# Sliding-window attention and token MLP: softmax terms of two row groups interleaved in memory, masks moved to GpSimd as 4-byte products, normalise allowed on GpSimd

## The chip, the cores and the metric

One core of one Trainium2 chip. The metric is device time in microseconds (us) of one execution. A kernel is timed in rounds beside the kernel before on the same chip, and every ratio below is the mean time of one kernel's fast runs over that of the other's fast runs of the same rounds, with its 95% interval, so it is not quite the ratio of the medians that are quoted. A kernel counts as faster or slower if that interval lies wholly beyond 2%, as the same if wholly within, and as unclear otherwise. One profiled execution of each kernel gives its trace. A run of this program on one core can also come out slow at a lower granted TensorE clock (`dense_wrong`: 521.8 us at a clock of 0.944, its three other runs 512.56 to 516.25 us at 0.954 to 0.963); only fast runs are compared, and it is said where a profile fell into the slow state.

## The reference, cut to what matters

```python
def _A_ref(x, wqkv, wo):                       # attention, 32 heads of 16, window 256
    B, S, D = x.shape                          # 1, 2048, 512
    H = 32; Dh = D // H; W = 256
    ...
    scores = jnp.einsum("bhqd,bhkd->bhqk", q, k) * (Dh ** -0.5)
    idx = jnp.arange(S)
    mask = (idx[:, None] - idx[None, :] >= 0) & (idx[:, None] - idx[None, :] < W)
    scores = jnp.where(mask[None, None], scores, -1e9)
    p = _softmax(scores, axis=-1)
    o = jnp.einsum("bhqk,bhkd->bhqd", p, v)
    ...
def _B_ref(x, w1, b1, w2, b2):                 # MLP over the tokens, 2048 -> 1792 -> 2048
    ...
def reference(A_x, A_wqkv, A_wo, B_x, B_w1, B_b1, B_w2, B_b2):
    x = A_x
    x = x + _A_ref(_layernorm(x, axis=-1), A_wqkv, A_wo)
    x = x + _B_ref(_layernorm(x, axis=-1), B_w1, B_b1, B_w2, B_b2)
    # ... and both once more with the same weights
```

## The kernel before: the parts that matter

The kernel is a list of 2,531 operations on five engines. The order in which they are issued, and the engine for those that may run on several, is a packed table made offline (`ORDER`); each operation carries an estimated `cost` that the offline search used and the chip never sees. `op("vector:mask", ..., alts=[("gpsimd", ...)])` means VectorE or, if the table says so, GpSimd.

Scores of eight heads (four row groups, `r` = 0 to 3, of two heads each) are made by four matmuls for each block of 64 keys, into four PSUM banks; most tiles hold two or three blocks. Two exponentials on ScalarE, each over a pair of banks (`i` = 0, 1; up to 512 columns each), write bf16 into a tile `pt` in SBUF, one row group after the other. Masks set the terms outside the window to zero by a product with 0/1, in place. Then eight small matmuls for each block take `pt` as the moving operand ("probability matmuls" below).

```python
pt = sb("pt", [P, NPT, 4, 512])                # bf16: tile, row group, column
...
op("scalar:exp", lambda e, ...: e.activation(
    pt[:, tp.slot, 2 * i:2 * i + 2, 0:cols], pair(ts)[:, :, 0:cols],
    ACTF.Exp, scale=SMSCALE), reads=[ts, "acttab"], writes=[(tp, i)], cost=act_cost(2 * cols))
...
def f_mask(e, ...):
    v = pt[:, tp.slot, :, c0 * 64:c0 * 64 + w]
    msk = ldm[:].rearrange("p a b -> p (a b)")[:, w0 * 64:w0 * 64 + w]
    if n == 1:
        return e.tensor_tensor(v, v, msk.unsqueeze(1).to_broadcast([P, 4, w]), op=ALU.mult)
    ...
nm = 4 * n * nc_ * 64
op("vector:mask", f_mask, reads=keys + LD, writes=keys, cost=dve_cost(nm, 0.5), lock=True,
   alts=[("gpsimd", f_mask, 100 + 2.03 * nm)])
...
last = e.matmul(..., lhsT=vb[...], rhs=pt[64 * h:64 * h + 64, tp.slot, r, base + c0 * 64:base + (c0 + n) * 64], ...)
...
def normalise(t):                              # (x - mean) * root, 512 columns, bf16
    op("vector:xh", lambda e: e.tensor_scalar(xh_sb[:, t, :], x_sb[:, t, :], agg[:, t, 0:1], rstd[:, t, :],
                                           op0=ALU.subtract, op1=ALU.mult), ..., lock=True)
```

The softmax here doesn't subtract the row's maximum and nothing guards it: scores larger than these inputs give would overflow.

## Time and profile before

| | kernel before |
|---|---|
| median of the first 3 runs | 479.63 us (478.91 to 480.4) |
| span of the profiled run, granted clock | 476.5 us, 0.988 |
| exponentials back to back, start to start | 0.904 us for 1,024 elements a partition |
| GpSimd mask back to back, 512 / 256 elements | 1.13 / 0.63 us |
| VectorE mask back to back, 512 elements | 0.34 us (mean duration 0.60) |

"Start to start" is the median spacing from an instruction to the next one on the same engine, taken where the engine was idle for under 30 ns between them; it is what an instruction costs its queue. A recorded duration is longer than that (here by some 25 to 140 ns): the records of neighbours overlap, as with the full-size exponentials of before, recorded at a mean of 1,054 ns and 904 ns start to start.

One line of the page of the kernel before gives the busy time of each engine in us, its share of the span and its instructions (PEld is TensorE's weight load, DVE VectorE, ACT ScalarE, POOL GpSimd):

```profile
PE 421.0 (88%) x6355; PEld 199.2 (42%) x6416; DVE 368.0 (77%) x702; ACT 331.4 (70%) x388; POOL 227.6 (48%) x252
```

By groups of instructions the page gives: line, engine, operation, output and inputs, shapes, count; then busy us and mean ns of one; then the idle time of that engine just before them and what ended most of it:

```profile
L685 ACT ACTIVATE pt<-PS 128x1024 bf16<-128x1024 f32 (+1 forms) x304 | 283.3, 1043 | 27.1 <-PE PS L670 26.4
L695 POOL TENSOR_TENSOR pt<-pt,ldm 128x256 bf16<-128x256 bf16 (+1 forms) x148 | 147.4, 1006 | 74.3 <-ACT pt L685 62.3
L695 DVE TENSOR_TENSOR pt<-pt,ldm 128x512 bf16<-128x512 bf16 (+1 forms) x124 | 69.7, 569 | 9.1 <-ACT pt L685 7.4
...
L493 DVE TENSOR_SCALAR xh_sb<-x_sb,agg,rstd 128x512 bf16<-128x512 bf16 x64 | 34.9, 561 | 2.2 <-POOL rstd L486 2.0
```

L685 is the exponential, L695 the mask, L493 the normalise. Two ways of masking share the work, 148 on GpSimd and 124 on VectorE (four more, for the tail, are on another line).

The chain of work that ended last, as shares of the span by engine:

```profile
PE 50%; DVE 30%; ACT 15%; POOL 2%; issue 2%; DMA 0%
```

Busy times of each engine in four stretches (columns: TensorE matmul, TensorE weight load, VectorE, ScalarE, GpSimd, then granted clock, DMA share and rate). The first and third are attention, the second and fourth MLP:

```profile
22.00:185.00 163.00, 134.66 (x2752) 61.52 (x2752) 149.21 (x266) 138.69 (x157) 105.91 (x110) 0.98 0.25 59
185.00:245.00 60.00, 58.29 (x404) 29.14 (x409) 39.82 (x86) 22.14 (x32) 7.33 (x9) 1.00 0.40 112
245.00:400.00 155.00, 138.05 (x2613) 61.62 (x2637) 133.53 (x248) 141.50 (x158) 101.19 (x108) 0.99 0.21 53
400.00:477.00 77.00, 72.50 (x331) 32.69 (x336) 27.78 (x48) 9.31 (x14) 1.47 (x2) 0.99 0.50 145
```

In the first attention stretch VectorE is nearly full (149 of 163 us); in the second ScalarE is fullest. The MLP stretches belong to TensorE (busy for 58.3 of 60 and 72.5 of 77 us). Of the table of waits (who waited for whom: us in total, times, longest), two lines of the kernel before:

```profile
POOL pt L695 <- ACT pt L685: 62.3, 39, 5.0
...
ACT pt L685 <- PE PS L670: 26.4, 40, 1.8
```

ScalarE waits 26.4 us for scores in all; that is how much faster exponentials could be fed at most.

### The profile page before, as it was taken

Reading aid. Unit: us, or ns where it says so; the run is one execution under the profiler, and the core shown is the slowest. Engines: PE = TensorE matmul, PEld = TensorE weight load, DVE = VectorE, ACT = ScalarE, POOL = GpSimd, SP = SyncE. Lnnn points to the kernel's source line nnn. Section 1 sums busy time; section 2 is a strip of 40 time slices with the busy share of each in tenths; the row PEclk is TensorE's granted clock in tenths of the full one; section 3 lists DMA queues with packets and bytes.
Section 4 is the critical chain, followed back from the end, with each engine's and each line's share of the span. In section 5 each row is a group of like instructions: output and inputs, shape, how many; then the busy total and the mean of one; then the engine's idle time right before and its main releaser. Section 6 shows DMA issues by size and latency. Waiting matters only on the chain.

```text
span 476.5 us, 14658 instructions
## 1 busy us (share of the span) xinstructions
PE 421.0 (88%) x6355; PEld 199.2 (42%) x6416; DVE 368.0 (77%) x702; ACT 331.4 (70%) x388; POOL 227.6 (48%) x252
## 2 busy tenths in 40 slices
...
GB/s 220 136 46 62 144 1 36 126 44 3 3 45 34 92 46 227 165 96 11 89 89 14 91 35 3 3 135 46 3 36 89 47 105 183 132 192 142 100 194 71
DMA packets 79392, 39.77 MB, mean 83 GB/s; under 512 B 20960, under 2 KB 79328, under 8 KB 79328
## 3 DMA queue, kind: packets, MB, share of 16 engines
...
## 4 chain that ended last, share of the span: by engine, by line
PE 50%; DVE 30%; ACT 15%; POOL 2%; issue 2%; DMA 0%
PE PS L512 30%; ACT pt L685 14%; DVE pt L695 8%; PE PS L837 7%; PE PS L670 4%; PE PS L607 4%; PE PS L716 4%; DVE rl L736 3%; DVE xh_sb L493 3%; DVE stats L470 2%; DVE x_sb L758 2%; DVE oT L747 1%; DVE vb L618 1%; POOL pt L695 1%; PE PS L514 1%
## 5 line engine op out<-in xcount | busy, mean ns | idle before, releaser
L685 ACT ACTIVATE pt<-PS 128x1024 bf16<-128x1024 f32 (+1 forms) x304 | 283.3, 1043 | 27.1 <-PE PS L670 26.4
L695 POOL TENSOR_TENSOR pt<-pt,ldm 128x256 bf16<-128x256 bf16 (+1 forms) x148 | 147.4, 1006 | 74.3 <-ACT pt L685 62.3
L695 DVE TENSOR_TENSOR pt<-pt,ldm 128x512 bf16<-128x512 bf16 (+1 forms) x124 | 69.7, 569 | 9.1 <-ACT pt L685 7.4
L512 PE MATMUL PS<-xh_sb,w1b 128*128 128x512 bf16 x262 | 69.2, 389 | 7.4 <-issue 2.4
L670 PE MATMUL PS<-qT,kbd 32*128 32x256 bf16 (+4 forms) x1488 | 61.4, 255 | 12.1 <-DVE rl L736 3.6
L512 PE MATMUL PS<-uT,w2b 128*128 128x512 bf16 x268 | 68.4, 379 | 0.9 <-issue 0.6
L486 POOL TENSOR_TENSOR rstd<-rstd,mhalf 128x2 f32<-128x2 f32 (+1 forms) x33 | 23.3, 712 | 78.5 <-DVE rstd L484 77.0
L864 DVE SCALAR_TENSOR_TENSOR x_sb<-PS,b2col,x_sb 128x512 bf16<-128x512 f32 x32 | 23.3, 747 | 47.8 <-PE PS L512 47.7
L716 PE MATMUL PS<-pt,vb 64*32 64x320 bf16 (+4 forms) x2976 | 44.9, 251 | 16.5 <-DVE pt L695 9.0
L512 PE MATMUL PS<-xhT,wqkv 128*128 128x512 bf16 (+1 forms) x218 | 51.6, 364 | 5.3 <-issue 2.2
L670 PEld LDWEIGHTS PS<-qT,kbd 32*128 32x128 bf16 x1488 | 22.1, 93 | 66.9 <-ACT pt L685 40.7
L852 ACT ACTIVATE uT<-rl,b1col 128x512 bf16<-128x512 f32 x28 | 18.3, 712 | 42.5 <-DVE rl L848 42.5
L736 DVE STREAM_TRANSPOSE rl<-PS 128x1024 f32<-128x1024 f32 x32 | 39.7, 1242 | 8.1 <-PE PS L716 7.8
L470 DVE BATCH_NORM_STATS2 stats<-x_sb 128x6 f32<-128x512 bf16 x64 | 42.9, 681 | 3.3 <-DMA x_sb<-in_A_x_dram 2.8
L716 PEld LDWEIGHTS PS<-pt,vb 64*32 64x32 bf16 x2976 | 28.5, 90 | 35.9 <-issue 11.2
L512 PE MATMUL PS<-uT,pt 128*128 128x512 bf16 x165 | 42.2, 379 | 0.2
L512 PEld LDWEIGHTS PS<-xh_sb,w1b 128*128 128x128 bf16 x280 | 23.0, 99 | 39.1 <-issue 11.1
L512 PEld LDWEIGHTS PS<-uT,w2b 128*128 128x128 bf16 x278 | 25.9, 98 | 31.6 <-issue 2.5
L837 PE MATMUL PS<-xh_sb,w1b 128*128 128x512 bf16 x165 | 37.1, 379 | 1.4 <-DVE xh_sb L493 1.2
L493 DVE TENSOR_SCALAR xh_sb<-x_sb,agg,rstd 128x512 bf16<-128x512 bf16 x64 | 34.9, 561 | 2.2 <-POOL rstd L486 2.0
L742 POOL TENSOR_TENSOR ul<-rl,rc 128x512 bf16<-128x512 f32 x23 | 25.8, 1123 | 22.3 <-DVE rc L740 20.5
L607 PE MATMUL PS<-wqkv,xhT 128*64 128x256 bf16 x512 | 34.0, 275 | 1.3 <-DVE rstd L484 1.3
...
## 6 DMA issues: line engine op xcount, KB each, us to landing
w1b<-in_B_w_dram SPq DMA_DIRECT2D x112, 128.0 KB, 2.7
...
```

Source lines behind the costliest of these rows:

```text
L470: op("vector:stat", lambda e: e.bn_stats(stats[:, t, :], x_sb[:, t, :]), reads=[f"x{t}"], writes=[f"st{t}"], cost=dve_cost(512), after=lat ...
L486: op("gpsimd:rstd", lambda e: e.tensor_tensor(rstd[:, t0:t1, 0], rstd[:, t0:t1, 0], mhalf[:, 0:1].to_broadcast([P, t1 - t0]), op=ALU.pow), ...
L493: op("vector:xh", lambda e: e.tensor_scalar(xh_sb[:, t, :], x_sb[:, t, :], agg[:, t, 0:1], rstd[:, t, :], op0=ALU.subtract, op1=ALU.mult), ...
L512: return e.matmul(o, lhsT=w, rhs=x, start=start, stop=stop, skip_group_check=True)
L607: last = e.matmul(bank(ft)[64 * j:64 * j + 64, sc * 256:(sc + 1) * 256], lhsT=xhT[:, tx.slot, c, tok:tok + 64], rhs=wqkv[:, c, 1024:1536]. ...
L670: last = e.matmul(bank(tt[r // 2], r % 2)[:, base + c0 * 64:base + (c0 + n) * 64], lhsT=kbd[32 * r:32 * r + 32, tk.slot, o, jj].rearrange( ...
L685: op("scalar:exp", lambda e, ts=ts, tp=tp, i=i, cols=cols: e.activation(pt[:, tp.slot, 2 * i:2 * i + 2, 0:cols], pair(ts)[:, :, 0:cols], A ...
L695: return e.tensor_tensor(v, v, msk.unsqueeze(1).to_broadcast([P, 4, w]), op=ALU.mult)
L716: last = e.matmul(bank(t, h)[32 * r:32 * r + 32, i + q0 * 64:i + (q0 + n) * 64], lhsT=vb[64 * h:64 * h + 64, tk.slot, jj, 4 * o + r, :], r ...
L736: op("vector:od", lambda e, t=tod, tr=tr: e.transpose(rl[:, tr.slot:tr.slot + 2].rearrange("p a b -> p (a b)"), pair(t)), reads=[(tod, i) ...
L742: f_n = lambda e, tr=tr, tl=tl: e.tensor_tensor(ul[:, tl.slot].rearrange("p (q x d) -> p x q d", x=2, d=16), T(tr)[:, :, :, 0:16], R(tl).u ...
L837: last = e.matmul(bank(tu, tt), lhsT=v()[:, sc - b0, k0 + tt * P:k0 + (tt + 1) * P], rhs=xh_sb[:, sc, :], start=(sc == b0), stop=(sc == NT ...
```

## The change

Its intent: put two row groups beside each other in memory, so that the bf16 terms of two heads at one column form one 4-byte word with one mask value, and mask both by one int32 product with 0 or 1. Then a mask costs GpSimd half as many elements, all 276 masks go there and VectorE gets rid of them. Normalise may now run on GpSimd, and the table was searched anew offline.

```diff
-    '...'        # ORDER, the packed table: replaced whole (35 lines, cut)
+    '...'
-        ldm = sb("ldm", [P, 4, 64])
+        ldm = sb("ldm", [P, 4, 64], dt.int32)
...              # the memset of the value tile's ones is written as 4-byte words; runs three times, at the start
         def normalise(t):
-            op("vector:xh", lambda e: e.tensor_scalar(xh_sb[:, t, :], x_sb[:, t, :], agg[:, t, 0:1], rstd[:, t, :],
-                                                   op0=ALU.subtract, op1=ALU.mult),
-               reads=[f"x{t}", f"ag{t}", f"rs{t}"], writes=[f"xh{t}"], cost=dve_cost(512, 0.25, ptrs=2), lock=True)
+            f_xh = lambda e: e.tensor_scalar(xh_sb[:, t, :], x_sb[:, t, :], agg[:, t, 0:1], rstd[:, t, :],
+                                             op0=ALU.subtract, op1=ALU.mult)
+            op("vector:xh", f_xh, reads=[f"x{t}", f"ag{t}", f"rs{t}"], writes=[f"xh{t}"], cost=dve_cost(512, 0.25, ptrs=2),
+               lock=True, alts=[("gpsimd", f_xh, pool_cost(512, 2))])
...
+        def probs(t):
+            return pt[:, t.slot].rearrange("p a b -> p (a b)").rearrange("p (i c r) -> p i c r", i=2, r=2)
...
-                            pt[:, tp.slot, 2 * i:2 * i + 2, 0:cols], pair(ts)[:, :, 0:cols],
+                            probs(tp)[:, i, 0:cols, :].rearrange("p c r -> p r c"), pair(ts)[:, :, 0:cols],
...
-                            v = pt[:, tp.slot, :, c0 * 64:c0 * 64 + w]
-                            msk = ldm[:].rearrange("p a b -> p (a b)")[:, w0 * 64:w0 * 64 + w]
+                            v = probs(tp).bitcast(dt.int32)[:, :, c0 * 64:c0 * 64 + w, 0]
+                            msk = ldm[:].rearrange("p a b -> p (a b)")[:, w0 * 64:w0 * 64 + w].unsqueeze(1)
                             if n == 1:
-                                return e.tensor_tensor(v, v, msk.unsqueeze(1).to_broadcast([P, 4, w]), op=ALU.mult)
+                                return e.tensor_tensor(v, v, msk.to_broadcast([P, 2, w]), op=ALU.mult)
...
-                        op("vector:mask", f_mask, reads=keys + LD, writes=keys, cost=dve_cost(nm, 0.5), lock=True,
-                           alts=[("gpsimd", f_mask, 100 + 2.03 * nm)])
+                        op("gpsimd:mask", f_mask, reads=keys + LD, writes=keys, cost=100 + 2.03 * 2 * n * nc_ * 64)
...
-                                            rhs=pt[64 * h:64 * h + 64, tp.slot, r, base + c0 * 64:base + (c0 + n) * 64],
+                                            rhs=probs(tp)[64 * h:64 * h + 64, r // 2, base + c0 * 64:base + (c0 + n) * 64, r % 2],
```

The exponential walks its output row group by row group (`p r c`), so it writes 512 bf16 elements at a step of 4 bytes, and then the 512 between them. The probability matmuls read at the same step.

More of the change, by code (lines that the diff above doesn't have):

```diff
@@ L15 @@
 ORDER = (
-    'c-qZXO=#mt7B1P9v>GZ<feI*44H{5`1{6?(2GpPhHK;)i8t{M`)Sv-1n8gF`#SLn3gBHA?0S&0Z4Ic0z3tsR-',
-    '7P63o7QB#y4?bid10Kl12M^@n1s`(AA%`5iu;t%4{WH^ZSax3=>D7;_>V5BfUkR;*!~noQ08sqB83aPn&|KiUnp6170YHM2iDEu7OJ&n4KKA?O',
-    '=_%!<sMe9H)vELa!u@h(Jh?7RMuAnnaD3Zx3$EpyfYDf%sogX*O%OzayOhAXpj<1$ktiM>3}1-',
-    'CxG%O&vKP<4`R2KJ@2Su}Oly%rjjApP!ZY}+EX#`Qrm1WsiJ2HC3H%2SY_+0EB0m9u?pT(Oh~H@N{P(BCymIONOcVuj&=!u)Yr~<U43v5p3O&O',
-    'x!eW;BLBHQGwx24*v)?otZ%$9sAKL9U#u(IUD0w{=@#y=?zmGF~^p@Z-h7g8E6vatw3<hz0=u>LcUXI5-Tat=p>8G-',
@@ L21 @@
-    'k1sObapLx5k`=Zm_m*ssqZ8Xvp?VFbMt%-',
-    '=P6VnXnb5!~2dAU?k6zS>L+gMiJ!eG#oudpbJzGxVDZ!~&fS&H(LX&U=mO`$F!9IHx<R8^gXQG`N_$|@@Qfuc~V={tn*J48G<*xkL>uJ*|VAq*',
-    '^{$ZDFBQ&p+yx~?ce&>8q!n$`e~v~};^ZX=2!N0KDnxOZ?*Py|U<cp{3FiZUh&&x>LxN#pTYy}TUpiXy80vt5P`Pdf;J4iMVDAhh?Hp{*^1&;g',
-    '3$*!QccSGUqq7&eRTcC+;DpOBn3d2#Yuj_WD)aNLfa0U<A60&@N8RfWd2QjO>NF!cR!Jg$bSB!%*L{EWB7NaQ8geN=hmW}Zu_@0a{iP?o<gInK',
-    'j}I{Q(cC$etqI?rQFc>(bgG~s1Qz1$ULIZ0Byb4sdGSSU!+KTV$)qPV-OD0eab3{yk}!LnEf(yp$kJQ2n$VgSana?W2|T;Ksdr<5{pXNOmRM(7',
@@ L26 @@
-    'No9sZ=pR_%7XDbL5pe>=AAs_nY1@87mstuieg(eG+Sx*s*A@Ku<mX&8o4tn0NJPBg4ir5Z*i<|R}vshT(#rjHP^PK~lGN!H%p-',
-    'UDHXkSt=X_Ita>s-',
-    'm(=K}3`d1+mzJ?Yk}}l4uc=Y*Vw+ZaXaPMAdd;72Ares0x}IPXQ3AyuH0m>G{RQiPS6bosKNsMJI?S1U5!@@4~4mQ5MG+ldCMLw)t-',
-    'LsL_WQv+f|^vEnMQ;E4!Q2z82~&O@jcTvPW{ElE^`hn@fn0>O<23?Yz;AW&^jEtx?<bqcZw1QAlP(*ej31fnS>p`I&gQq9psLWw5&Y@hx8=;#R',
-    'f2qTISWN1mAVa5W~2xi-',
-    'r%5G8898J?0L(P(YJ<z?r;vvA2a%!4Xf)Mbq&hvfHYzEC{v(t&=lM_gUxQeS)R>|!t986{)AD2pEwTMaB910MZwj2*`99a;6mTB8ilQm6-',
@@ L32 @@
-    'BA}lOfWy|*s8B-',
-    '4wy$_hCY~3t0)K+e0SLyI1N(GhU)Y9Ga2)4L*LA_=rT$PK4v(9c!{P5bXMP6yo+r!EzV?qs;<^>E7w;9@64@uT!CzlrJ)jDd!F};QW~b|QS-Lp',
-    'f?+d5;2_vN1!GuMK4kfXPnBEP?gDB#t>q02S<FUCbLOA%z7Pc4))Du`$=*ZApYRe>7yIVWkLL@{)QPA-',
-    '0k0Cl4jYlu;eFh{Rz&6@q+3oduq<e5oNc*4-LJZ2aTCE)JhZ~jR-Hm$P_k95B_3uCmVxP%mo#{rS&XlYv%NYkkP(z|5#!CF^)petOVOgWcFJDz',
-    'EmD<V4399tEwJ4svwyf;3np7-GE0t>WBK}voQhym%V;zlLRCN+mRFtUdR-',
-    '>xtk*^ANsq7R1C_NQ{%{xz2l@<yfKB5>u@!Shz{A45+tG4a?rcZrO1z*@&q0@0Szu9zruW8wJuciowV){P(qU6e^ISj)hEcSzv_h6`MXJ?w!-',
@@ L38 @@
-    ';<<Xk7+<xx-Vsa@2cuw&2zVPbeNfcR)atdS}g;oncqlA%5IX^_19HxjQA0%#g-',
-    'M7*uyH9eR^<kV17MhS0Z^@f9kW^qj6ktTsL&B!|d=#ah$)jf@1Lav1yu$LxRAz3$Cs^b`VIeXqt{anIOmYToX^V<!5zp9R#qC_V#*;r|khK8}}',
-    'tchXf01Qv)Q5WDNnn3@@kZtEvMCguwuvoopFfSI2^ojYfOh+f11t4;t)}Jnjq+&$A>+4iB;{WBT*<u%5ns0|7_LIXaI3&zI9ms}k^EYIRF174_',
-    '*Kc&MunRCe1i8taDc`-',
-    'W*iD7qq5R45l14Ya!x$>cc3HG}c@>gocFMe&kd35xgma6Gg}BUT69?hikn$!CSrA7$AFhgLh2Bw0RacYEC?tY=Noc#9cl*`2eSqzU^r7G$9sfD',
-    '(X#;CoE7u*HgTNB}nQ><H&PqhF8bd&kG7s<N90?_$8hg&Q0Nx;_RRK<p-',
@@ L44 @@
-    'xA$zju1t0)`Fz8&PRFmbvmnAmJikt@nMuNcci(Sy|9qWD&rj^jI#Sp;6je%l2Ol*AL!`SmNFdV~nOsAk%&1z-',
-    'Tg@CB4LJLfeV^Og|1b}Inq9~~vbVUyoRMS=_6OS_Cwl$PxB00RWWSNLe`Q+XN7?@>7o?uq{0A&0C47%|pKe|5PkB*Y4a}u}P5i7%NkR-KcD!9k',
-    'T`)ZaIqQiQW@U>>G6V(}LtvV<(2PcUX!&-',
-    '`xBtooq%O$TQ?7MyeIuJ`94qa@TKvOkU6>J;KOjUuR;Hf8oPqAE%<JOuS;O6aR=dIBX8^_IN%_hRNe)vuYgkZe~F1La6ZD*bQtP|#$j<0rSkNo',
-    '_T*(;w1ca}@uS$pU6w~xiz`PnN!|K9{)6XbK7o9qP^11k_%6VA?;oBGT)bGKp2gIkl=Hk(e|$ldr0Omg|$Er{mPGPtL~&Lf`#Jp~-',
-    'j+mM?tzgTIGD#rnCeWCm^Iox7o8Xvb<X+3v~<)?$(uOu=*3kcrs0}D8E%$>bw{``bXH$MX-',
@@ L50 @@
-    'H$QRieRAE3Kesy9P2>!c4;+kJJ=cO?MR()8$3*TO%6<ZUf2-v_S_U&jxZJy8FqGaqDz~bb1sj&RyQ!y-',
-    '#_*AtxR3b%JG+y=b5o)q|2{Wz??F22%;h$7OPkGHG&iTVV&#m58*}327A3f`<mjA^(<vKMTf)LzZpq7;^uV?HT9p1w2H3!yp38EbXJt{ROTA-',
-    '4wGslj6rH8^aQS7_^P<gjD_xpT%Y$`YV=HY=HEPz_T!OL*=5jR$;wF+skkgJ;=OS7*bz>n&tD%jVznVLBz;c0&>F6w)Tn^@zQq8;>5HpmxRWZX',
-    '^W2s+o`unAuVO5fOZk@IH_jKk12I0m$8S|{<euZo+xy>&=c=s&%{0HSCw_Y$S{p8-4lEr1TuDl#rSEo-',
-    'bJ??{3xLeo6I~#JV<8Z4hkz1c~b5X1~yLv9QhFhL`xx@!_B=<`K2Y#c#%vr;6pYS>NaiRV%N!d*@KdPW>0CBg`zG2D#h1UKDY!*cW'
+    'c-pO2F^KcX6&}g*?kwns`C$%pph5>aP+$%eP(TL?D4;?YRH)E_0xnc2;D8GSeBi<a1sqV}LWK(-IN*Q-',
@@ new lines @@
+    'E>yU1z=Z=_Y+wT$@WCFqaIuAp4LIOp16yn$PhNZN{qMg^Nd9L_8a=%k&HLti-zY{M{F@p=$aNjZaRn4bk>`1V_j51!5(x-',
+    'tSO+t7HAimRNtL$x=_5*hEm)eSGqzZ0%awfVFFn~)rqlY>rLHKZZpL+mH3eP5B9??g6h&EbrI6N>ysLp-',
+    '|8<#lGws&aI+JTl|6`k){jV)mu2b4kSsJTfsj8`3QmsZ!(_{vvcB8SNDj|rFNEFHC<pajs_2nhJ;G4yhL>TjZX{6D0L4P&~f(G^Tn?)8oPEkw?',
+    '+nN;PtI<cpp>L`RC8N<eALqFlm}K+YEcd*h{GB*X@@+yE$#tV?lc*QDZXDN1oe)zC)f#cW)CY=UM;6SdqogT7ks7ISb90$JW`^BrU3Ltk-',
+    'G<~%vlT_A%2*sLVdy78z=SKkt!aj)hoNml`U2;=%VqIN>rPi)OPfc%xB1)E#~)u^UFmwLz11{DQB~E@G{yqN9N!kfp@c$UD~hrCXk!?%EHgshh',
@@ new lines @@
+    '@z^l*iyaKw0lh}ih}9jeli|SMH_1mms)$?>aE_`*`LH;wiQW~7^76PZTeG~r*3NM@0bFniyBpQRhBh)?bi2Ix%B>o=tQ40%bHF;|7^RZqme}EN',
+    'YuzTgMO0KhT$+GSyqT{yKjhM*6DQeZnu*GIE-bKev+oX-',
+    '|P3N>wY0zI3BJISGAqRV9^}UW=;*W&=;{AsDTgkb4MdvwG+qg+P0x5$p$M}cDxX~PuQ~Nib^T|=t6@OnYL9FrYV5K-',
+    'JPnbKrvjeU(M%o<WAh4EYm-WgteH+8o$>y9UhCC>q34&W|3{zYh!H~ez3T^lVlnGRFK}#@f2@1;s%4QR{3PIoGfo!DDN$MGS0B)-',
+    'L&U356=jpq!{-yu#2qQ9cH4~>$Q8mUY@rpAR*SpIB6!5NE5@L#H!U8VBq+HZ$XN%sM-ZlV7|+q&_gwyQU>eHs4g(2Dl{5cjv<6vmd&sMWyW-eX',
@@ new lines @@
+    '|6-',
+    'S3ez&nD}iMa){r@=Vtj!K3?|Fg9a(KQgh;YP$R(ak7K`b$%*9jb7)=IX9VqlEhmyS6L?~%AkO&Up3Qm$IiWYGOy`dYqq3GMbYluvQkwsMHg2b;',
+    '2$P?QwnaD^Ks|a}PY4f>=3;+~X0_fsTv7DwdRctBGC0*}NK{v)@)3}wGBgyb8UoHyWg49DooW!<!kfdl5cn=6o4Th)zGlTnJZQC|zi>b;6k{(r',
+    '6+9((!v|KJ_Vi-*D>cYGaW)u?u;#2c;BD9gTO(zq`1TC(UIBH(cW_4*ci{r^8t#Swr#$(iXtB#v-',
+    'j$?TMBSIHH_Pi_ucpL#q4Z!26QJx#zza+!h7!uM$Nz(lFno{a*VcKE128-fIyF|)ja(~kb++<V?{Rv_t7Dc+=L7|>O$!qO+JQ@JF0?-',
+    'Qu0i^&SEGtq`0~DZSvJ8ZDLAV$)9?3uN14Y$5dS{S3rdhzEzlk6ef*`5V^g%7{X_fV#o?4kC>v|L59gXVs{?`WTd5A$p5c#&Q>kFo7#7FU!Oao',
@@ new lines @@
+    'b$JueJ@5mNf_pt|n8s!~OfB!pI%mzS%Rx<c;qw%>Q%JpTe?38*xi&+5OL75W6$WUPs!VGINSJsosrvn=Ztd66Xlz;8BC>w|vUhhxCCyTZ8JT`v',
+    '2b{>|f~AUtMy-T@(4PbQ!awvC3PPKQlDo25OJ!v>J&tyU(~5P*4q-|ZkFO}nuE%@CB+sHck3Xy^({8}&{tq$%-',
+    'QK^O+GE&=|F|3zGn6DV@~4{|*jSu&^?s?}rnX@l;8E0$qemSNm3sIFh@x}|kG^VzKPIs0n18O<iF7|+HCT@^)391PNQB$h=n&|;9q=@eu@%=0c',
+    'Dj=IBcw?7Pmpx@KpbdZ>~TIm}}YBu3@NmtAo4Z{rDsR$8z=-Y-7aF`G)^sT_hLDl8xTiv15@rM$~8u}4K0xb15-',
+    'jZ*PJA!m|0o#MoRV_=kY)e##DHEbFggDtL*5djBh$2%7UEkg+iK1N3=MR!ZgsLE*;o#<GQL-',
@@ new lines @@
+    'G(=NoA~$oj)^G0u8DgoeXmn&(*x>eOtuTCH{~Z9}(|G<qZmeAv!>%c{Adz<|dFbK=<deaEsKW>|(BhK$3wt+-',
+    'OT<+c^5H%g6WbGuz{IBB)rhGD#2$MI?<aefH<==GI(v$&yv?|kkUic$>F*TC$q44XiAGL+>$5G0j>-bvDKcQh>#DTxuRAADorC;|<jRFbe-wL#',
+    'luj1>J7;5#PQm-',
+    '87ETq$#J3BKsAm)R;cbRRxZ;4$Vv5e)>}qJk}RS|ZVov^diuwRxSU>pK);EO7N~2ymjX7S<YW=+^Qu>^AD{c0GvIAXF3#j5AI6<k<j;J>Rr!J9',
+    'U6DCKeQg#zLu#X<H=<d~-+<u0t8r?0}#N!4yYiNdv>k8x5#wEW6Bc1Yu+<m@KCcg9Q}W6UG4wHbQSJ+}%GQ*d&I-',
+    '<z#U+bXjR@1Epz05PGcNlcH$^2{ht3xw*Md*2P`Y)uKVCGwzJQilS2=jnaM;JCQSSilmNOaf}qj1-',
@@ new lines @@
+    '>bY1)pt_Cg~uH5*U;`$W4i>MB!73pbu``s|#E?j@zH#XF_=h-',
+    '*pS80mt!x06WKSxO0xHRCevk`Dy3M?hkf;XuP)bSJCL~`NHo{{BsN3mCDJ8!anfq?48kgz5-T;@GqX@fG;EPl`7Al-',
+    'ajX?_i=m)l2G>LPkZv^eHq0)2MWBv?ZXeR;-6725vuHgK?krahb4GM@MI03Sx)=e!*Pd*AGF;R_AA3bPj&a(wO=94@8*4y2!F`^6obRe-XYLov',
+    'SsjrHryeJ)9(DMyOTJMJJOBgP7^!2zn{9_vC2tm{0FX<awYlqAi%w_e1CA<`zHBLa@_a7hx;J2{cxG@YO_+Qyn}RQ$J(=fQJ(EsRXI}Wg-',
+    '1|^JCdCp2?dSn{&}@*@Kw0%n&oxptwIF!tDcTj`k#ILGosbf_&p1&)xGYNorT@qUV|`)U?17bk+3UX;V5al26ujxnlkYGAZh1EDcVPzmtb(vhG',
@@ L55 @@
+    'XaAju9s!byhh$@UgN(;aQH(jxe5`q2uqRAGmjOuO6|kR;#ClU48ZFRoNee=1|f+|B~w~A>T_6NELTVyB$Vc35T%PseO-',
+    '<)bB8W<4!h^%0VQ4kVuuo5d8a#b2sgsI-h9IUSv;Yi9c#T{~z}_?)5EyO!-w2b4NLQUl#ALCyx7Wk-',
+    'zSLs){H2{ruoXFODks60{eTm(wfn$>z<yY~4SAJ^x>Q2z)qE`F}Kw`v4Nhy?gU|MY#8DFWd*7-T!L;2Jsd+U;'
 )
@@ L460, in bass_interleave_layers__sliding_block__mixer_token_mlp__prompt_kernel @@
         ONES = [("one", i) for i in range(3)]
+        two_ones = 1.0 + 0x3F80 / 2.0 ** 23
         for i in range(3):
-            op("gpsimd:one", lambda e, i=i: e.memset(vb[:, i, :, :, 16:32], 1.0), reads=["mhalf"], writes=[("one", i)], cost=1750,
-               alts=[("vector", lambda e, i=i: e.memset(vb[:, i, :, :, 16:32], 1.0), 1700),
+            f_one = lambda e, i=i: e.memset(vb[:, i].bitcast(dt.float32)[:, :, :, 8:16], two_ones)
+            op("gpsimd:one", f_one, reads=["mhalf"], writes=[("one", i)], cost=950,
+               alts=[("vector", f_one, 1150),
                      ("scalar", lambda e, i=i: e.activation(
```

4 lines of the change are left out of this document (1 added, 3 removed).

## The prediction

> **What bounds the kernel now.** By the busy times of windows, 185–245 and 400–477 us are TensorE-bound (58.3 of 60, 72.5 of 77 us) and hardly touched. In the first attention window (22–185 us) VectorE is fullest (149.2 of 163 us), then ScalarE 138.7, TensorE 134.7, GpSimd 105.9; in the second (245–400) ScalarE leads (141.5 of 155), TensorE 138.1, VectorE 133.5, GpSimd 101.2. ScalarE is mostly the 304 exponentials, which follow each other at 904 ns start to start: 152 x 0.904 = 137 us per layer. ScalarE's waits for score matmuls are 26.4 us (table of waits; 15.4 and 10.5 by layer). That is the stock to win.
>
> **What changes.** All 276 masks go to GpSimd, over half as many elements. Groups by shape: VectorE loses 58.8 + 11.1 + 1.8 = 72 us. On GpSimd a back-to-back 512-element mask starts every 1.13 us, a 256-element one every 0.63 us: 1.96 ns an element plus 0.13. If int32 costs as bf16 does, the halved masks cost 0.63 and 0.38 us: about 192 x 0.63 + 80 x 0.38 + 5 = 156 us (as busy time about 180, against 152 now). The new order, read against the old operations, puts 36 of 64 normalises on GpSimd (estimate 0.75 us each from the 0.67 us one-pointer multiply: +27 us; VectorE -18), and returns 10 key multiplies and 6 products to VectorE and 7 evictions from ScalarE to VectorE (+14 us VectorE, -3 us ScalarE). VectorE: 368 to about 285 us; GpSimd: 228 to about 265; ScalarE 328; TensorE unchanged.
>
> [...] VectorE's 512-element masks average 598 ns, but 343 median back to back; normalise 561 against 323. [...] with VectorE masks gone, much of this goes.
>
> **Strides.** Exponentials now write, and probability matmuls read, bf16 at a 4-byte step. [...] I expect exponentials at 904 ns and the same matmul times. No run here shows it yet.
>
> **Critical path.** Of the chain of waits, masks take 9% and normalise 3%; but the waits move. With VectorE near 70% and GpSimd near 75–80% of the attention windows, ScalarE becomes the bound. Its window from first to last exponential is about 166 us in the first layer and 148 in the second, with floors near 150 and 142 (exponentials plus evictions): at most some 16 + 6 us. I expect about two thirds, mostly in the first layer.
>
> **Predicted: 465 us**, 458 to 475 in 8 of 10. Faster by over 2%: 0.65; within 2%: 0.31; slower: 0.04.
>
> **What would show each step.** Halved GpSimd masks near 0.63/0.38 us start to start (wrong: int32 slower); exponentials still 904 ns; probability matmuls unchanged; VectorE below 300 us; its remaining normalises near 0.35 us; ScalarE's waits for scores well under 26 us; first attention window shorter by over 8 us, second by under 8.
>
> **What would make it wrong.** An int32 product at over 3 ns an element would put GpSimd above 300 us and make it the bound. A strided exponential write at half rate would add over 100 us. GpSimd's queue is in order: a product or reciprocal root behind masks delays the output projection and normalise. The chain may turn to TensorE earlier than I think (138 of 155 us in the second window), or the new order, made offline, may leave ScalarE idle at chunk ends.

The sum came to 465 us: two thirds of at most 16 + 6 us, off the 479.6 us of before. That queues are in order the traces of before and after do show: GpSimd's instructions (252 and 398), VectorE's (702 and 563) and ScalarE's (384 and 377 that name a tile) start in the program's order there, without exception.

## The result

The changed kernel takes **553.77 us** median (551.79 to 554.88, 4 runs) against 480.01 us before: ratio 1.152, 95% interval 1.1455 to 1.1585. It is 15% slower, where 3% faster was predicted. The lines of the changed kernel that answer to those above (L688 exponential, L698 mask, L492 normalise), first the busy times:

```profile
PE 441.7 (80%) x6352; PEld 203.6 (37%) x6412; DVE 310.0 (56%) x563; ACT 402.6 (73%) x381; POOL 315.2 (57%) x398
```

VectorE lost 58 us of busy time as intended. ScalarE, on which nothing was meant to change, gained 71, and GpSimd 88. The groups:

```profile
L688 ACT ACTIVATE pt<-PS 128x1024 bf16<-128x1024 f32 (+1 forms) x304 | 357.4, 1404 | 15.8 <-PE PS L673 14.2 <-PE PS L716 0.7
L698 POOL TENSOR_TENSOR pt<-pt,ldm 128x256 int32<-128x256 int32 (+1 forms) x272 | 176.5, 663 | 87.9 <-ACT pt L688 82.1
L492 POOL TENSOR_SCALAR xh_sb<-x_sb,agg,rstd 128x512 bf16<-128x512 bf16 x36 | 75.7, 2107 | 1.3
...
L492 DVE TENSOR_SCALAR xh_sb<-x_sb,agg,rstd 128x512 bf16<-128x512 bf16 x28 | 16.3, 585 | 14.8 <-POOL rstd L485 14.6
```

Here are both surprises. The same 304 exponentials have a mean duration of 1,404 ns in place of 1,043. And a normalise takes 2,107 ns on GpSimd, where the prediction put 0.75 us. The masks are close to plan: 0.69 and 0.42 us start to start for 256 and 128 elements, estimated at 0.63 and 0.38.

The profiled run's granted TensorE clock was 0.960, against 0.988 before, and TensorE's busy time was 441.7 us against 421.0, for about as many matmuls (6,352 recorded, against 6,355). What part of the loss goes by way of this clock wasn't separated. It comes with the edits tested below and goes with them: `flat_addmul`, which undoes two of them, has a clock of 0.996 and a busy time of 420.8.

The chain of work that ended last has turned from TensorE and VectorE to ScalarE:

```profile
ACT 51%; PE 29%; POOL 13%; DVE 5%; issue 2%; POOLq 0%
```

The corresponding stretches (22 to 205 and 270 to 460 us are attention here):

```profile
22.00:205.00 183.00, 136.50 (x2658) 61.76 (x2677) 117.10 (x201) 175.04 (x159) 140.20 (x175) 0.94 0.19 46
205.00:270.00 65.00, 56.96 (x346) 25.25 (x350) 35.68 (x67) 14.59 (x21) 17.71 (x14) 0.95 0.41 114
270.00:460.00 190.00, 150.63 (x2686) 67.68 (x2708) 109.86 (x198) 180.92 (x163) 134.94 (x180) 0.96 0.18 41
460.00:550.00 90.00, 80.89 (x465) 36.36 (x474) 32.61 (x54) 15.33 (x21) 11.88 (x11) 1.00 0.48 139
```

ScalarE is now 95% busy in both attention stretches, 175 of 183 and 181 of 190 us, with about as many instructions as before (159 and 163, against 157 and 158). And the waits:

```profile
POOL pt L698 <- ACT pt L688: 82.1, 73, 4.9
...
ACT pt L688 <- PE PS L673: 14.2, 14, 4.0
...
PE PS L837 <- POOL xh_sb L492: 5.9, 2, 4.4
```

ScalarE itself waits less for scores than before (14.2 us against 26.4), while GpSimd's masks wait longer for exponentials (82.1 against 62.3). What exponentials wait for comes sooner, and what waits for them waits longer. From the first to the last exponential the first layer took 166.2 us before and 196.2 after, the second 159.0 and 188.6: together 59.6 us of the 73.6 us by which the span grew. Another 9.3 us lies between the last exponential of the first layer and the first of the second (59.3 to 68.6), where MLP matmuls wait for normalises on GpSimd (L837, the last line above).

Runs of exponentials in the timeline (start, length, then the instructions merged; the line's length includes the tail of its last one). The kernel before, then the changed one:

```profile
289.40 23.29 ACT L685 ACTIVATE pt<-PS 128x1024 bf16<-128x1024 f32 x25
```

```profile
291.96 8.94 ACT L688 ACTIVATE pt<-PS 128x1024 bf16<-128x1024 f32 x8
```

25 in 23.29 us are 0.93 us each; 8 in 8.94 us are 1.12 us each. Start to start, the medians over the whole run are 0.904 us (254 pairs) and 1.154 us (279 pairs): 0.25 us more for each, times 292 full-size exponentials, is 73 us of ScalarE's queue. So far this is arithmetic that fits; whether the write's step makes exponentials slow, and what the time would be without it, is for experiments.

### The profile page after: what moved, and what is told of

It is laid out like the page before. It is cut to its first block, busy times and chain, and to the rows that moved or that the text cites. A ratio compares the mean times of both kernels' runs of the same rounds, so it can differ in the third digit from the quotient of the medians.

```text
span 550.1 us, 14628 instructions
## 1 busy us (share of the span) xinstructions
PE 441.7 (80%) x6352; PEld 203.6 (37%) x6412; DVE 310.0 (56%) x563; ACT 402.6 (73%) x381; POOL 315.2 (57%) x398
## 4 chain that ended last, share of the span: by engine, by line
ACT 51%; PE 29%; POOL 13%; DVE 5%; issue 2%; POOLq 0%
ACT pt L688 50%; PE PS L515 18%; POOL xh_sb L492 7%; PE PS L837 6%; POOL pt L698 4%; PE PS L673 2%; PE PS L610 1%; DVE stats L469 1%; PE PS L716 1%; POOL rstd L485 1%; DVE rl L736 1%; DVE x_sb L758 1%; ACT kbd L583 1%; PE PS L517 0%; PE PS L551 0%
## 5 line engine op out<-in xcount | busy, mean ns | idle before, releaser
L688 ACT ACTIVATE pt<-PS 128x1024 bf16<-128x1024 f32 (+1 forms) x304 | 357.4, 1404 | 15.8 <-PE PS L673 14.2
L698 POOL TENSOR_TENSOR pt<-pt,ldm 128x256 int32<-128x256 int32 (+1 forms) x272 | 176.5, 663 | 87.9 <-ACT pt L688 82.1
L515 PE MATMUL PS<-xh_sb,w1b 128*128 128x512 bf16 x256 | 67.9, 391 | 11.8 <-issue 3.7
L492 POOL TENSOR_SCALAR xh_sb<-x_sb,agg,rstd 128x512 bf16<-128x512 bf16 x36 | 75.7, 2107 | 1.3
L716 PE MATMUL PS<-pt,vb 64*32 64x320 bf16 (+4 forms) x2976 | 47.6, 259 | 24.9 <-POOL pt L698 15.7
L515 PE MATMUL PS<-uT,w2b 128*128 128x512 bf16 x255 | 63.7, 379 | 0.6 <-issue 0.3
L515 PE MATMUL PS<-xhT,wqkv 128*128 128x512 bf16 (+1 forms) x239 | 58.8, 373 | 6.1 <-ACT pt L688 3.3
L837 PE MATMUL PS<-xh_sb,w1b 128*128 128x512 bf16 x165 | 40.8, 400 | 7.1 <-POOL xh_sb L492 5.9
L610 PE MATMUL PS<-wqkv,xhT 128*64 128x256 bf16 x512 | 38.5, 293 | 1.6 <-ACT stg L594 1.0
L515 PE MATMUL PS<-wo_sb,oT 128*128 128x512 bf16 x118 | 31.8, 387 | 2.5 <-DVE rc L740 1.1
L515 PEld LDWEIGHTS PS<-xhT,wqkv 128*128 128x128 bf16 x258 | 22.7, 102 | 29.3 <-issue 6.5
```

What stands on the lines that cost most here:

```text
L492: f_xh = lambda e: e.tensor_scalar(xh_sb[:, t, :], x_sb[:, t, :], agg[:, t, 0:1], rstd[:, t, :], op0=ALU.subtract, op1=ALU.mult)
L515: return e.matmul(o, lhsT=w, rhs=x, start=start, stop=stop, skip_group_check=True)
L610: last = e.matmul(bank(ft)[64 * j:64 * j + 64, sc * 256:(sc + 1) * 256], lhsT=xhT[:, tx.slot, c, tok:tok + 64], rhs=wqkv[:, c, 1024:1536]. ...
L688: op("scalar:exp", lambda e, ts=ts, tp=tp, i=i, cols=cols: e.activation(probs(tp)[:, i, 0:cols, :].rearrange("p c r -> p r c"), pair(ts)[: ...
L698: return e.tensor_tensor(v, v, msk.to_broadcast([P, 2, w]), op=ALU.mult)
L716: last = e.matmul(bank(t, h)[32 * r:32 * r + 32, i + q0 * 64:i + (q0 + n) * 64], lhsT=vb[64 * h:64 * h + 64, tk.slot, jj, 4 * o + r, :], r ...
```

## The experiments

**Theory.** An exponential that writes at a 4-byte step is slow by itself, and this is most of the loss; GpSimd's slow normalise is a smaller, separate one. **Rivals.** (A) The new order with all masks in one engine's queue is slow. (B) The exponentials are slowed by what GpSimd or TensorE does to the same memory. (C) GpSimd's normalises are the main cause. (D) Any walk that isn't contiguous on both sides costs as much. (E, F) come with their runs.

The kernel before ran beside each set, at 478.6 to 479.9 us median.

### First set: undo one part of the change at a time

`dense_wrong`: the changed kernel's order, engines and element counts, but exponentials and matmuls use the contiguous layout of before. The int32 product then pairs neighbouring columns, which is wrong at the mask's edge.

```diff
-    probs(tp)[:, i, 0:cols, :].rearrange("p c r -> p r c"), pair(ts)[:, :, 0:cols],
+    pt[:, tp.slot, 2 * i:2 * i + 2, 0:cols], pair(ts)[:, :, 0:cols],
-    v = probs(tp).bitcast(dt.int32)[:, :, c0 * 64:c0 * 64 + w, 0]
+    v = pt[:, tp.slot].bitcast(dt.int32)[:, :, c0 * 32:c0 * 32 + w // 2]
-    rhs=probs(tp)[..., r // 2, ..., r % 2]
+    rhs=pt[..., tp.slot, r, ...]
```

> The changed kernel with its order, its masks on GpSimd and its int32 products over as many elements, but the exponentials written and read contiguously (the product then pairs neighbouring columns, so the result is wrong at the mask's edge, on purpose). Theory (the 4-byte step of the exponential's write costs 250 ns each): exponentials back to 904 ns start to start, time falls by 60 to 75 us to 480-495 us. Rival A (the new order and the all-GpSimd masks lengthen the chain): exponentials may change, but the time stays above 520 us. Rival B (exponentials are slowed by GpSimd's many int32 accesses, not by their own step): exponentials stay near 1150 ns and the time stays near 553 us.

Measured: 513.33 us over the three fast runs (514.79 over all four), ratio 1.0717 (1.0649 to 1.0785), result wrong. Exponentials are back to exactly 904 ns start to start. Rival B in the form "GpSimd's int32 accesses slow them" falls: those are all still there. But the time fell by 40 us, not by 60 to 75: my expectation missed, and something else holds the kernel well above before.

`dense_wrong_xh`: the same, and the 36 normalises that GpSimd did are back on VectorE, at the same places of the order.

```diff
-    lock=True, alts=[("gpsimd", f_xh, pool_cost(512, 2))])
+    lock=True, alts=[("vector", f_xh, pool_cost(512, 2))])
```

> As dense_wrong, and the 36 normalises that GpSimd does at 2.05 us are back on VectorE, same order. This is the change as the prediction costed it, without the two costs that it did not foresee. Theory: 462 to 474 us, exponentials 904 ns, normalises 0.3 to 0.6 us. Rival A: above 490 us.

Measured: 488.92 us, ratio 1.0219 (1.015 to 1.0288; unclear at 2%). 24 us came from normalise, but 488.9 lies between what the theory (462 to 474) and rival A (over 490) expected: neither is borne out here.

`xh_dve`: that last edit alone, on the changed kernel, right result.

> The changed kernel with its 36 GpSimd normalises back on VectorE, same order, strided exponentials kept; result right. Theory: GpSimd's 76 us of normalises cost 10 to 20 us of the time (mostly between the attention stages, where matmuls wait for them), so 533 to 545 us, exponentials still 1150 ns. Rival C (the slow normalises on GpSimd are the main cause): below 510 us.

Measured: 544.35 us, ratio 1.1344 (1.1279 to 1.141), result correct, exponentials 1,156 ns. As the theory expected; rival C (normalise is the main cause) falls. While exponentials are slow, taking the normalises off GpSimd gives 9 us; once they are fast, 24. The two costs hide each other in part.

`flat_write`: the changed kernel's layout, but each exponential walks in memory order of its output. It writes contiguously and reads alternately from its two PSUM banks. Right result.

```diff
-    probs(tp)[:, i, 0:cols, :].rearrange("p c r -> p r c"), pair(ts)[:, :, 0:cols],
+    probs(tp)[:, i, 0:cols, :], pair(ts)[:, :, 0:cols].rearrange("p r c -> p c r"),
```

> The changed kernel with each exponential walking its elements in memory order of its output: contiguous write, and reads that alternate between two PSUM banks. Same layout, result right. Theory (the write's step is what costs): 904 to 950 ns, and the time falls to 480-500 us. Rival D (any walk that isn't contiguous on both sides costs as much): exponentials at 1100 ns or more, time near 553 us or above.

Measured: 518.45 us, ratio 1.081 (1.0733 to 1.0888), correct. Exponentials: 904 ns. Their group, and one of their runs in the timeline, 6 in 5.60 us:

```profile
L688 ACT ACTIVATE pt<-PS 128x1024 bf16<-128x1024 f32 (+1 forms) x304 | 283.0, 1040 | 54.8 <-PE PS L673 53.9
```

```profile
323.63 5.60 ACT L688 ACTIVATE pt<-PS 128x1024 bf16<-128x1024 f32 x6 [0.66 <-PE PS L673]
```

This settles the first surprise. Same bytes in the same places, same readers, same masks; only the order in which one instruction visits them is different, and 250 ns of each exponential are gone. Rival D falls too: alternating between two PSUM banks costs nothing that can be seen (904 ns both ways). The time again missed my 480 to 500 us. In this kernel GpSimd has taken ScalarE's place in the chain of work that ended last, next to TensorE:

```profile
PE 40%; POOL 34%; ACT 14%; DVE 8%; issue 2%; DMA 1%; SPq 0%; POOLq 0%
PE PS L515 24%; POOL pt L698 17%; ACT pt L688 14%; POOL xh_sb L492 10%; PE PS L837 6%; PE PS L673 3%; PE PS L716 3%; PE PS L610 3%; POOL rstd L485 2%; POOL kbd L596 2%; DVE rl L736 1%; DVE stats L469 1%; PE PS L517 1%; POOL ul L742 1%; POOL
```

GpSimd's masks (L698) and normalises (L492) are 27% of the chain; in the changed kernel GpSimd had 13% in all.

### Second set: the costs by themselves

`forms`: why is a normalise on GpSimd 2.05 us, when a multiply by one per-partition value of the same 512 elements (the key multiply, 25 of them in this kernel) is 0.67? The changed kernel with normalises dealt out over five lines; each line has another form, and the result is wrong.

```diff
+    o, x, m, s = xh_sb[:, t, :], x_sb[:, t, :], agg[:, t, 0:1], rstd[:, t, :]
+    f_xh = [lambda e: e.tensor_scalar(o, x, m, s, op0=ALU.subtract, op1=ALU.mult),      # L496, as in the change
+            lambda e: e.tensor_scalar(o, x, s, m, op0=ALU.mult, op1=ALU.add),           # L497
+            lambda e: e.tensor_scalar(o, x, m, 1.0, op0=ALU.subtract, op1=ALU.mult),    # L498
+            lambda e: e.tensor_scalar(o, x, s, 0.0, op0=ALU.mult, op1=ALU.add),         # L499
+            lambda e: e.tensor_scalar(o, x, s, m, op0=ALU.mult, op1=ALU.subtract)][...] # L500
```

> The changed kernel with its normalises dealt out over five forms, on five lines, so that GpSimd runs some of each (result wrong on purpose): subtract a per-partition mean then multiply by a per-partition root; multiply then add, both per-partition; subtract a mean then multiply by 1; multiply by a root then add 0; multiply then subtract, both per-partition. Theory (the second per-partition operand is what costs): the three forms with two such operands near 2.05 us, the other two near 0.67 us. Rival E (the subtraction costs): forms with a subtraction near 2.05 us, multiply-then-add with two operands near 0.75 us.

Measured, the groups of this kernel on GpSimd (mean ns is the number after the busy time):

```profile
L500 POOL TENSOR_SCALAR xh_sb<-x_sb,rstd,agg 128x512 bf16<-128x512 bf16 x9 | 18.7, 2082 | 0.1
...
L498 POOL TENSOR_SCALAR xh_sb<-x_sb,agg 128x512 bf16<-128x512 bf16 x7 | 14.2, 2023 | 0.2
...
L496 POOL TENSOR_SCALAR xh_sb<-x_sb,agg,rstd 128x512 bf16<-128x512 bf16 x6 | 12.6, 2099 | 0.4
...
L499 POOL TENSOR_SCALAR xh_sb<-x_sb,rstd 128x512 bf16<-128x512 bf16 x8 | 5.7, 709 | 0.4
L497 POOL TENSOR_SCALAR xh_sb<-x_sb,rstd,agg 128x512 bf16<-128x512 bf16 x6 | 4.8, 798 | 0.1
```

Rival E is right and my theory wrong. Each form with a subtraction takes 2.0 to 2.1 us, with one or two per-partition operands, in either place; without one, a second per-partition operand costs 0.09 us (798 against 709). The time of this kernel, 541.38 us, is one run and not compared.

`before_write`: the other way round, the kernel before with the 4-byte step put into the exponentials' write alone (full tiles, 292 of 304). Its readers keep the old addresses, so the result is wrong; order, masks and engines are those of before.

```diff
-    pt[:, tp.slot, 2 * i:2 * i + 2, 0:cols], pair(ts)[:, :, 0:cols],
+    probs(tp)[:, i, 0:cols, :].rearrange("p c r -> p r c") if cols == 512 else
+    pt[:, tp.slot, 2 * i:2 * i + 2, 0:cols], pair(ts)[:, :, 0:cols],
```

> The kernel before, its order, masks and engines unchanged; only the exponentials of full tiles write at the 4-byte step (the readers still take the old addresses, so the result is wrong on purpose). Theory: exponentials near 1150 ns start to start with nothing else changed, 530 to 545 us. Rival B (exponentials were slowed by what GpSimd or TensorE does to the same memory): exponentials stay at 904 ns and the time at 480 us.

Measured: 529.77 us, ratio 1.1045 (1.1007 to 1.1084), a hair under the range I gave. Full-size exponentials 1,150 ns start to start; the twelve smaller ones, not touched, keep 690 and 477 ns as before. The group of all 304:

```profile
L688 ACT ACTIVATE pt<-PS 128x1024 bf16<-128x1024 f32 (+1 forms) x304 | 356.3, 1402 | 8.0 <-PE PS L673 7.4
```

With no new order, no int32 and no normalise on GpSimd, the write's step alone costs 50 us. Rival B falls for good.

`before_read`: the kernel before with only the probability matmuls' reads of full tiles at the 4-byte step; wrong result.

```diff
-    rhs=pt[64 * h:64 * h + 64, tp.slot, r, base + c0 * 64:base + (c0 + n) * 64],
+    rhs=probs(tp)[64 * h:64 * h + 64, r // 2, base + c0 * 64:base + (c0 + n) * 64, r % 2] if tp.cols == 512 else
+        pt[64 * h:64 * h + 64, tp.slot, r, base + c0 * 64:base + (c0 + n) * 64],
```

> The kernel before with only the probability matmuls' reads of full tiles at the 4-byte step (wrong result on purpose). Theory: matmul times unchanged (mean 251 ns for the group), time within 1% of before. Rival F (strided reads slow the matmuls): group mean above 275 ns and time above 488 us.

Measured: 480.05 us, ratio 0.9994 (0.9947 to 1.0041). The group of probability matmuls, in the kernel before and here, has a mean of 251 and 252 ns:

```profile
L716 PE MATMUL PS<-pt,vb 64*32 64x320 bf16 (+4 forms) x2976 | 44.9, 251 | 16.5 <-DVE pt L695 9.0
```

```profile
L719 PE MATMUL PS<-pt,vb 64*32 64x320 bf16 (+4 forms) x2976 | 46.0, 252 | 17.0 <-DVE pt L698 9.7 <-DVE agg L472 2.1 <-DVE uT L830 1.5
```

The ends of matmuls are modelled in a profile, so the time of the kernel is the firmer evidence. The same 4-byte step that costs ScalarE 250 ns in a write costs TensorE nothing that these runs can see in a read (ratio 0.9994). Rival F falls.

`flat_xh`: `flat_write` with all normalises on VectorE, a right result without either surprise.

> The changed kernel with the contiguous write of flat_write and all normalises on VectorE: right result, without the two unforeseen costs. From dense_wrong_xh (489 us) and the 4 us between flat_write and dense_wrong: 488 to 496 us. If the order's own cost (+9 us over before, still unexplained) is due to the wrong layout's different results, it falls to 480 us or less instead.

Measured: 490.71 us, ratio 1.021 (1.0164 to 1.0255; unclear at 2%), correct. So the layout is not what keeps `dense_wrong_xh` at 489; the remaining 11 us over before come from the order with normalises on an engine that it wasn't made for, or from masks that all queue on GpSimd. The next run tells these apart.

### Third set: the change as it was costed, and a version with the order of before

`flat_addmul`: `flat_write` with normalise left on GpSimd, but without a subtraction: one more small VectorE instruction per group makes the negated mean, and normalise adds it, then multiplies.

```diff
+    def f_var(e):
+        e.tensor_scalar(nmean[:, t0:t1, 0], agg[:, t0:t1, 0], -1.0, 0.0, op0=ALU.mult, op1=ALU.add)
+        return e.tensor_scalar(rstd[:, t0:t1, 0], agg[:, t0:t1, 1], a, b, op0=ALU.mult, op1=ALU.add)
...
-    f_xh = lambda e: e.tensor_scalar(..., agg[:, t, 0:1], rstd[:, t, :], op0=ALU.subtract, op1=ALU.mult)
+    f_xh = lambda e: e.tensor_scalar(..., nmean[:, t, :], rstd[:, t, :], op0=ALU.add, op1=ALU.mult)
```

> The changed kernel with the exponentials' contiguous write, and its 36 GpSimd normalises kept on GpSimd but as add then multiply (of a negated mean, made by one more small VectorE instruction per group), which the run of the five forms puts near 0.75 us in place of 2.05. Result right. This is the change as the prediction costed it, with both unforeseen costs gone. If only those two were wrong in the prediction: 460 to 475 us. If all masks on GpSimd in this order cost time on their own (matmuls wait 30 us for GpSimd's masks in flat_xh, at 490.7): 480 us or more.

Measured: **472.31 us**, ratio 0.9856 (0.9828 to 0.9883), correct: the change becomes a gain of 1.4%, clear of noise but under the 2% that count as faster. Its normalises on GpSimd and its exponentials:

```profile
L692 ACT ACTIVATE pt<-PS 128x1024 bf16<-128x1024 f32 (+1 forms) x304 | 282.0, 1048 | 19.8 <-PE PS L677 18.7 <-PE PS L720 0.4
...
L496 POOL TENSOR_SCALAR xh_sb<-x_sb,nmean,rstd 128x512 bf16<-128x512 bf16 x36 | 28.9, 804 | 1.3
```

0.80 us of duration and 0.74 start to start, as the prediction costed it. These two edits alone make the 81.5 us between this and the changed kernel. So rival A falls: with the engines it was searched for, the new order with all masks on GpSimd does not lose time against before, and putting its GpSimd normalises on VectorE (`flat_xh`) throws 18 us away.

`pairs_f32`: the kernel before with its own order and its own split of masks, plus the pairs in memory by contiguous writes, and each mask one product over half as many elements as fp32 numbers times 1.0 or 0.0. I took it that a pair of bf16 seen as one fp32 number comes out of a product with 1.0 unchanged, on either engine. The result was right with 148 such masks on GpSimd and 124 on VectorE; whether the product is exact was not tested.

```diff
-    ldm = sb("ldm", [P, 4, 64])
+    ldm = sb("ldm", [P, 4, 64], dt.float32)
-    v = pt[:, tp.slot, :, c0 * 64:c0 * 64 + w]
+    v = probs(tp).bitcast(dt.float32)[:, :, c0 * 64:c0 * 64 + w, 0]      # exponentials as in flat_write
```

> The kernel before, its order and its split of the masks between the engines, with pairs interleaved by contiguous writes and each mask one product over half as many 4-byte elements, as fp32 times 1.0 or 0.0 [...]. Result right. Expected: exponentials 904 ns; GpSimd's masks near 0.69 and 0.42 us in place of 1.13 and 0.63; VectorE's near 0.34 us as before[...]; time 470 to 478 us. If halving GpSimd's masks is worth nothing in this order: 480 us.

Measured: **468.42 us**, ratio 0.9786 (0.9767 to 0.9805), correct. It is the fastest kernel, 2.1% under before (unclear at 2%), and 1.6 us under the range that I gave. It is also 3.9 us faster than `flat_addmul` in the same rounds, with the old order and the old split of masks. So no run here shows that the new order, or moving all masks to GpSimd, was worth anything beyond the halved masks. Its masks:

```profile
L698 POOL TENSOR_TENSOR pt<-pt,ldm 128x128 f32<-128x128 f32 (+1 forms) x148 | 94.2, 644 | 106.7 <-ACT pt L688 92.9 <-DVE pt L698 11.7
...
L698 DVE TENSOR_TENSOR pt<-pt,ldm 128x256 f32<-128x256 f32 (+1 forms) x124 | 56.8, 464 | 10.2 <-ACT pt L688 8.6 <-POOL pt L698 0.8
```

GpSimd's 148 masks are down from 147.4 to 94.2 us of busy time (0.70 and 0.41 us each, start to start). VectorE's cost the same 0.34 us start to start as before (256 elements of 4 bytes take as long as 512 of bf16), but their mean falls from 569 to 464 ns and that of normalise from 561 to 471. In the trace of before, VectorE's 512-element masks average 412 ns where no GpSimd instruction ran at the same time and 724 where one did, and here GpSimd's masks are busy for 53 us less; that the one brings the other is likely, but was not isolated.

`before_steps`: how the write's cost depends on the step. As `before_write`, with an 8-byte step in full tiles (all four row groups interleaved); one look, result wrong on purpose.

```diff
+    def quads(t):
+        return pt[:, t.slot].rearrange("p a b -> p (a b)").rearrange("p (c i r) -> p i c r", i=2, r=2)
-    pt[:, tp.slot, 2 * i:2 * i + 2, 0:cols], pair(ts)[:, :, 0:cols],
+    quads(tp)[:, i, :, :].rearrange("p c r -> p r c") if cols == 512 else pt[...], pair(ts)[:, :, 0:cols],
```

> As before_write, with full tiles' exponentials written at an 8-byte step ([...]result wrong on purpose). If the cost grows[...]: near 1400 ns start to start or more. If any step beyond contiguous costs the same: near 1150 ns.

Measured: exponentials 2,275 ns start to start; the kernel took 849.24 us in its one run, whose granted TensorE clock was 0.783. That clock is no rival for the exponentials: the twelve that weren't touched keep 707 and 478 ns, as in `flat_addmul` (706 and 477) at a clock of 0.996. The group:

```profile
L691 ACT ACTIVATE pt<-PS 128x1024 bf16<-128x1024 f32 (+1 forms) x304 | 678.1, 2486 | 5.7 <-PE PS L676 5.5
```

The cost grows with the step: 904 ns contiguous, 1,150 at 4 bytes (27% more), 2,275 at 8 bytes (152% more). An estimate from these runs: count the bytes of the tile that an exponential passes over, each pass anew. One of 1,024 elements passes over 4,096 bytes at the 4-byte step (two passes of 2,048) and 8,192 at the 8-byte step; 1,150 / 4,096 and 2,275 / 8,192 are both 0.28 ns a byte. The smaller strided exponentials of the changed kernel fit too: 871 ns for 768 elements (3,072 bytes) and 573 ns for 512 (2,048 bytes) are 0.28 ns a byte. Contiguous, an exponential of 1,024 passes over 2,048 bytes, which would be some 0.57 us by this estimate, under the 904 ns that it takes; that may be why its write costs nothing extra, but it was not tested. The points agree with one constant; that bytes, and no larger unit, are what counts isn't shown by them.

### Fourth set: what is left, and the missing corner

Two things were still open: the 7 us between `flat_addmul` and the predicted 465, where the weight loads of the probability matmuls wait 25 us for GpSimd's masks, and how the loss divides between the two costs.

`split_third`, `split_half`: `flat_addmul` with fp32 masks, every third or every second of them on VectorE at the same place of the order.

```diff
-    op("gpsimd:mask", f_mask, ...)
+    masks[0] += 1
+    op("vector:mask" if masks[0] % 3 == 0 else "gpsimd:mask", f_mask, ...)       # % 2 in split_half
```

> flat_addmul with fp32 masks, every third of them on VectorE instead of GpSimd, same order, result right. If masks queueing on GpSimd are the rest of the gap: 464 to 469 us, and matmuls wait under 15 us for GpSimd's masks. If it is the order or TensorE: 471 to 475 us. [...]476 us or more.

> As split_third with every second mask on VectorE. Queueing theory: 464 to 471 us, no better than split_third[...]. Order theory: 471 to 475 us.

Measured: 517.13 us over the five fast runs of `split_third` (520.57 over all seven), ratio 1.0801 (1.0772 to 1.0831), and 534.85 us for `split_half`, ratio 1.1162 (1.1143 to 1.1181); both correct. No range that I gave holds either of them, but for the open one, "476 us or more". It stood for VectorE's masks slowing GpSimd's, a guess of mine; and the traces don't bear that out: GpSimd's masks of 256 elements take 753 ns in `split_half` and 755 in `split_third`, 747 in `flat_addmul`. So these runs can't say where the 7 us are. (The profile of `split_half` is used.) Three lines of its table of waits:

```profile
ACT pt L694 <- PE PS L679: 74.5, 75, 4.9
POOL pt L704 <- DVE pt L704: 71.3, 33, 6.9
...
DVE pt L704 <- POOL pt L704: 36.7, 25, 3.8
```

The masks of one tile follow each other, in this program, by semaphore. In `flat_addmul` one queue holds them all; here VectorE and GpSimd wait for each other (37 and 71 us). Where it was checked, both start their instructions in the program's order (GpSimd 252 of 252 and VectorE 702 of 702 in before); then what stands behind a waiting mask waits as well, until ScalarE starves for scores (74.5 us against 18.7 in `flat_addmul`). The split of `pairs_f32` is as even as this one, 148 to 124, and that kernel is fast; its order was searched with that split. That mutual waiting is the cause of the whole 62 us is an inference from this table, not a separate experiment.

`addmul`: the missing corner, the changed kernel with its strided write and the cheap normalise on GpSimd.

> The changed kernel with its strided exponential write, and the normalises on GpSimd as add then multiply of a negated mean (0.74 us in place of 2.05), same order and engines, result right. If ScalarE's slower exponentials hide most of GpSimd's excess: 530 to 542 us, so the write step alone is worth 58 to 70 us of the 74. If the two costs add up: 505 to 512 us (553.8 less 46).

Measured: 533.29 us, ratio 1.1132 (1.1076 to 1.1189), correct: the first expectation, that slow exponentials hide most of GpSimd's excess. Now the four corners are there, same order and engines:

| us, median | normalise subtracts (2.05 us) | normalise adds (0.74 us) |
|---|---|---|
| exponential writes at a 4-byte step (1.15 us) | 553.8 (the change) | 533.3 (`addmul`) |
| exponential writes contiguously (0.90 us) | 518.5 (`flat_write`) | 472.3 (`flat_addmul`) |

The write's step costs 35 us where normalise is slow and 61 where it is not; normalise 20 or 46. Together they cost 81.5 us, which is 25 less than the 107 that 61 and 46 would add up to. Slow exponentials would give GpSimd the time to catch up; that is an inference from the waits, in which GpSimd's masks wait 82.1 us for exponentials in the change and 51.0 in `flat_write`.

## Why the prediction was wrong, point by point

- *"I expect exponentials at 904 ns and the same matmul times"*: **the step that failed first.** They took 1,154 ns in the change and 1,150 in the kernel before with that one edit. By itself it costs 50 us in the order of before and 61 in the new one. The ground that the prediction gave was no run ("No run here shows it yet"). It had named the strided write as a risk ("would add over 100 us" at half rate), but gave slower a chance of 0.04. The same step in a read by TensorE costs nothing that can be seen (ratio 0.9994), so that half of the sentence was right.
- *"estimate 0.75 us each from the 0.67 us one-pointer multiply"*: **the second.** On GpSimd this normalise takes 2.05 us. The estimate counted operands, and in `forms` the operation is what matters (2.02 to 2.10 us with a subtraction, 0.71 to 0.80 without): with an addition in place of the subtraction it takes 0.74 us. The excess is 36 x 1.3 = 47 us of GpSimd's queue, and 20 to 46 us of the time.
- *GpSimd 265 us, ScalarE 328 us*: 315 and 403 measured; both misses are these two terms: in `flat_addmul`, without them, the engines are busy for 266.9 and 328.2 us.
- *Masks 0.63 and 0.38 us*: 0.69 and 0.42 measured, 10% more. The int32 product gave a right result in every run that kept the layout and wasn't wrong on purpose. Nor was it dearer than the fp32 product of `pairs_f32` (0.70 and 0.41); whether it is exact was not tested. The step per element is (689 - 416) / 128 = 2.1 ns. The bf16 masks of before, at (1,130 - 628) / 256 = 1.96 ns, are a little under it.
- *"With VectorE masks gone, much of this goes"*: wrong for the change. What VectorE has left is no faster than before: its 28 normalises average 585 ns against 561, and its 15 products `ul` (L742, the weighted values times the reciprocal sums) 889 against 709. In `xh_dve`, where GpSimd does no normalise, they average 488 and 715, so GpSimd's work is a likely cause; it was not isolated. VectorE's busy time fell to 310, not 285, and that was not followed up. What the trace of before shows: the 40 of VectorE's 512-element masks during which no GpSimd instruction ran took 361 to 426 ns (mean 412), the other 59 up to 1,845 (mean 724); 29 normalises without one took 365 to 414 ns (mean 400), the other 35 up to 1,319 (mean 694). A longer record also meets more of GpSimd's, so this alone doesn't give the cause. In `pairs_f32`, where GpSimd's masks are shorter, the mean of VectorE's fell from 569 to 464 ns.
- *The first attention window shorter by over 8 us, the second by under 8, ScalarE the bound*: ScalarE is the bound in the change (busy for 95% of both attention stretches), but each window is 30 us longer there, not shorter. Once the two costs are gone, the forecast lengths come out: from first to last exponential `flat_addmul` takes 156.3 and 158.9 us, against 166.2 and 159.0 before, and ScalarE is busy for 136.8 of 144 us (22 to 166) and 145.5 of 158 (228 to 386). Its chain that ended last is mixed, though: TensorE 43%, GpSimd 21%, ScalarE 21%. The prediction had a slip here: it gave the second window as 148 us, where the trace of before has 159.0 (235.2 to 394.2).
- *465 us*: with both terms repaired the change takes 472.3, inside the predicted range of 458 to 475. The two terms explain the loss, but not all of the miss: even without them the gain over before in the same rounds is 6.3 us, under half of the 14.6 forecast (479.6 to 465). That it lies in the range owes something to the range's width. Where the last 7 us are stays open: slower masks (10%) would be about 14 us of GpSimd's queue, and `split_third` and `split_half` failed to test it.
